# The bilinear MLP's last product summed over four chunks in PSUM, with two small edits of the planner's input

## The chip, the cores and the metric

One NeuronCore of a Trainium2 chip runs the kernel. The metric is the device time of one execution in microseconds, the median of several runs. Five engines work side by side, each through its own list of instructions in order: PE (matrix products), ACT and DVE and POOL (elementwise work), and SP, which here only issues DMAs.

## The reference

Inputs are q, k and v of 4 batches x 8 heads x 576 positions x 64, and phi of 4 x 8 x 576 x 32. The rest are weights. The output has 2304 tokens x 512.

```python
# attention over 32 memory slots
a = softmax of phi over the 576 positions
k_m = einsum('bhsm,bhsd->bhmd', a, k);  v_m = einsum('bhsm,bhsd->bhmd', a, v)
x = softmax(q @ k_m.T / 8) @ v_m               # heads side by side: 2304 x 512
# leaky MLP, 512 -> 2048 -> 512
h = x @ moe_w_in;  y = maximum(0.01 * h, h) @ moe_w_out
# bilinear MLP, 512 -> 1536 -> 512
out = ((y @ moe2_w_a) * (y @ moe2_w_b)) @ moe2_w_out
```

## The kernel before

All large products are fp32 by three passes: each operand is split into a high part (a cast to fp32r) and a low part (what the cast left), and PE multiplies high by high, low by high and high by low, summing in PSUM. So each weight has to be loaded, cleaned up and split before PE can use it, and each intermediate as well.

**A planner writes the order.** Every step is given to `Program.op` with its engines and estimated cost, the tiles that it reads and writes, how early it may be placed (`ahead`), how many places of its room it must leave free (`keep`), and a `slack` that moves its due time. `Program.order` then lists all of them for all engines, a step at a time, and assigns places: "slot" is a common room of SBUF tiles, which raw weights, products, accumulators and stored parts all share; "y" is a room of two PSUM banks. A tile gets its place when the one before it is done with. `SLACK` holds the slacks by kind.

**Stage 1** (to about 393 us) makes the attention and the leaky MLP. At its start SP issues the loads raw_win (first weights), phi, four kv (keys and values of the first batch, 512 of the positions for each half of the heads), kvr (the remaining 64 positions), q, and raw_wout. PE makes `km` from kv and from kvr (line 586), turns the result (`kvt`, 603), makes scores `sc` (674), and then `vw`, `h` (806) and `y` (836).

**Stage 2**, the bilinear MLP, goes through the tokens in two sweeps (s = 0 and 1), in each over 12 chunks c of 128 hidden columns. Tokens that don't fill the halves ("left") are done in the first sweep. For each chunk: raw_wa and raw_wb are loaded (`weight`, line 475), ACT splits off parts (481, 484), DVE cleans and joins them (488, 492, 496, 499), ACT casts the high half of the weight wo (404), DVE or POOL takes off the low half (1004); `w_sums` (987) makes wo number 2 and 3 as sums of them. Chunks 0 to 3 are prepared in stage 1 (`PRE`). All prepared weights are stored to device memory (k_wo, k_wout, and k_wf) and loaded again in the second sweep (1029). With them PE makes the two products for the halves as seven smaller ones (`ab_unit`, tiles abx, aby, abz, line 1049) and for the left tokens as `a` and `b` (`left_unit`, 1100). Their elementwise product is split into p (or pl for the left tokens).

`o_unit` is the last product, p times wout (the tile raw_wout, prepared the same way). One unit takes one quarter of the output columns (e) and one of three token groups (l: 0 and 1 the halves, 2 the left ones), and sums two chunks in one PSUM tile: 6 matmuls (line 1132). The first unit of a group of tokens and columns is copied into an accumulator in SBUF (oacc, oaccl), the others are added there by DVE (1145). After every odd chunk 12 such units go into a queue, from which 6 are placed in each chunk. In the second sweep, chunks below 8 use another form, `o_part` (PE tile os, 1248), which takes sums of wout (w2s, from stored parts wf) and whose first results are copied into osum.

Of the kernel before, what the change touches and what calls it, by code (L numbers as in the profile page):

```python
# [19 lines left out]
P = 128  # L20
# [32 lines left out]
SLACK = {'win0': 5.37, 'wout0': 8.13, 'win': 4.9, 'wout': 4.64, 'wa': 23.6, 'wb': -0.15, 'wout2': 16.8, ('sc', 0, 0): 6.2, ('sc', 0, 1): 3.3, ('sc', 1, 0): 8.05, ('sc', 1, 1): 6.75, ('sc', 2, 0): 11.99, ('sc', 2, 1): 9.96, ('vw', 0, 0): 19.04, ('vw', 0, 1): 7.99, ('vw', 0, 2): 9.35, ('vw', 1, 0): -0.31, ('vw', 1, 1): 19.18, ('vw', 1, 2): 8.18}  # L53
# [279 lines left out]
def tile_mem_attention__leaky_mlp__bilinear_mlp(  # L333
# [128 lines left out]
    def weight(kind, c, k, after=()):  # L462
# [62 lines left out]
        op(two(512), 0, lo, r=[a, ("hi", key)], w=[key], tiles=[cv, key], ahead=any_time, slack=SLACK[kind + "0" if first else kind])  # L525


    def kv_part(b, g):
# [4 lines left out]
        if b == 0:  # L533
            tile_of(phi, "slot", [1, S])
            op("DMA", c_dma(P * S * 4), lambda T: nc.sync.dma_start(T[phi], phiT[b, :, g:g + 1, :]), w=[("e", b, g)], tiles=[phi])
        elif g == 0:
            tile_of(phi, "big", [2, S])
            op("DMA", c_dma(P * S * 8), lambda T: nc.sync.dma_start(T[phi], phiT[b]), w=[("e", b, 0), ("e", b, 1)], tiles=[phi], keep=6)
# [7 lines left out]
        for i, k in enumerate(kvt):  # L546
            tile_of(k, "slot", [2, 512])
            op("DMA", c_dma(P * 4096), lambda T, i=i, k=k: nc.sync.dma_start(T[k], kv[b, g, :, 2 * i:2 * i + 2, :]), w=[k], tiles=[k], keep=6)
        if g == 0:
            tile_of(rest, "slot", [2, 512], parts=64)  # L550
            op("DMA", c_dma(64 * 4096), lambda T: nc.sync.dma_start(T[rest], kv_rest[b]), w=[rest], tiles=[rest], keep=6)
# [96 lines left out]
    def q_load(b, g):  # L648
        if b > 0:
            q = ("q", b, g)  # L650
            tile_of(q, "big", [2, S])
            op("DMA", c_dma(P * S * 8), lambda T: nc.sync.dma_start(T[q], qT[b, g]), w=[q], tiles=[q], keep=6)
            return
        for x in range(2):
            q, cols = ("q", b, g, x), slice(x * NB, (x + 1) * NB)
            tile_of(q, "slot", [2, NB])
            op("DMA", c_dma(P * S * 4), lambda T, q=q, cols=cols: nc.sync.dma_start(T[q], qT[b, g, :, :, cols]), w=[q], tiles=[q])
# [456 lines left out]
    def o_unit(s, c, l, e, pos):  # L1114


        size = NB2 if l < 2 else B * LEFT
        o = ("o", s, c, l, e)
        ps_ = [(("p", s, x, l), 0) if l < 2 else (("pl", c // 2), x % 2) for x in (c, c + 1)]
        ws = [("wout2", x, s) for x in (c, c + 1)]  # L1120
# [8 lines left out]
        def prod(T):  # L1129
            for x, ((g, at), w) in enumerate(zip(ps_, ws)):  # L1130
                for k, (u, v) in enumerate(PASSES):
                    nc.tensor.matmul(  # L1132
                        T[o], T[w][:, u, es], T[g][:, at, v, :], start=(x == 0 and k == 0), stop=(x == 1 and k == 2)
                    )

        op(
            "PE", 6 * c_pass(size), prod,
# [10 lines left out]
        if c == NC2 - 2:  # L1148
# [84 lines left out]
    def o_part(q, x, nth, pos):  # L1233
# [151 lines left out]
```

## Time and profile before

| | us |
|---|---|
| median of the runs shown | 806.5 |
| lowest and highest of 3 | 805.35, 806.81 |
| the profiled execution, its own time | 809.07 |
| span of that profile | 807.3 |
| PE busy | 784.9 |
| DVE busy | 667.7 |
| ACT busy | 375.8 |
| POOL busy | 215.2 |

The mean granted clock of PE in the profile is 0.987 of full speed. Busy times are sums over the span; where PE is full in a stretch, the other engines' idle time there costs nothing. A row of a timeline gives start, length, engine, line, and in brackets how long the engine was idle before and what ended that.

### The profile page before, as it was taken

Reading aid. Unit: us, or ns where it says so; the run is one execution under the profiler, and the core shown is the slowest. Engines: PE = TensorE matmul, PEld = TensorE weight load, DVE = VectorE, ACT = ScalarE, POOL = GpSimd, SP = SyncE. Lnnn points to the kernel's source line nnn. Section 1 sums busy time; section 2 is a strip of 40 time slices with the busy share of each in tenths; the row PEclk is TensorE's granted clock in tenths of the full one; section 3 lists DMA queues with packets and bytes.
Section 4 is the critical chain, followed back from the end, with each engine's and each line's share of the span. In section 5 each row is a group of like instructions: output and inputs, shape, how many; then the busy total and the mean of one; then the engine's idle time right before and its main releaser. Section 6 shows DMA issues by size and latency. Waiting matters only on the chain.

```text
span 807.3 us, 13391 instructions
## 1 busy us (share of the span) xinstructions
PE 784.9 (97%) x4898; PEld 700.0 (87%) x4898; DVE 667.7 (83%) x1273; ACT 375.8 (47%) x817; POOL 215.2 (27%) x328
## 2 busy tenths in 40 slices
PE   5889999999999999999999999999999989999998
PEld 4578889999999999999988888888888878878886
DVE  6898899889887988888768899889885676888975
ACT  5657776777565665654326534344321143222110
POOL 3462247215011411431100113056330000244300
PEclk9789999999999999999999999999999999999999
DMA  9885302064227133136887555646578778957302
GB/s 325 323 281 181 132 1 74 6 235 125 76 76 267 59 132 118 42 125 233 279 311 276 209 199 192 208 158 202 216 264 304 276 267 274 296 173 283 130 1 104
DMA packets 55218, 150.02 MB, mean 186 GB/s; under 512 B 6897, under 2 KB 20209, under 8 KB 55153
## 3 DMA queue, kind: packets, MB, share of 16 engines
q1 hardware_dynamic: 55152, 149.18, 53.4%
q8 instruction: 38, 0.62, 0.3%
q14 instruction: 28, 0.22, 0.1%
HBM read 103.55 MB, written 45.61 MB: 185 GB/s over the span
## 4 chain that ended last, share of the span: by engine, by line
PE 93%; DMA 3%; DVE 2%; issue 1%; ACT 0%; SPq 0%; DVEq 0%; ACTq 0%
PE y L836 26%; PE o L1132 13%; PE h L806 12%; PE aby L1049 12%; PE abz L1049 8%; PE abx L1049 8%; PE os L1248 4%; PE vw L757 2%; PE b L1100 2%; PE a L1100 2%; PE sc L674 1%; DMA kvr<-in_kv_rest_dram 1%; DMA k_wout<-wout 1%; PE km L586 1%; DMA raw_win<-in_w_in_dram 1%
## 5 line engine op out<-in xcount | busy, mean ns | idle before, releaser
L836 PE MATMUL y<-g,wout 128*128 128x288 f32 x1536 | 221.0, 297 | 0.0
L836 PEld LDWEIGHTS y<-g,wout 128*128 128x128 f32 x1536 | 210.8, 190 | 3.7 <-issue 1.7
L1049 PE MATMUL aby<-yb_T,wo 128*128 128x512 f32 x432 | 110.2, 390 | 0.5 <-DVE t L1057 0.5
L1049 PEld LDWEIGHTS aby<-yb_T,wo 128*128 128x128 f32 x432 | 80.1, 188 | 16.8 <-DVE t L1057 0.9
L1132 PE MATMUL o<-p,wout 128*128 128x512 f32 x384 | 94.0, 390 | 0.0
L783 ACT ACTIVATE g<-h 128x288 fp32r<-128x288 f32 x128 | 52.8, 413 | 70.1 <-PE h L806 64.4
L1132 PEld LDWEIGHTS o<-p,wout 128*128 128x128 f32 x384 | 71.9, 188 | 15.4 <-DVE osum L1145 0.3
L806 PE MATMUL h<-ahi,vwh 128*128 128x288 f32 x256 | 76.8, 300 | 1.2 <-ACT ahi L404 1.2
L1057 DVE TENSOR_TENSOR t<-aby,t 128x512 f32<-128x512 f32 x72 | 49.5, 688 | 34.2 <-PE aby L1049 32.4
L806 PE MATMUL h<-alo,vwh 128*128 128x288 f32 x256 | 76.1, 297 | 0.8 <-POOL alo L387 0.8
L806 PE MATMUL h<-ahi,vwl 128*128 128x288 f32 x256 | 75.9, 296 | 0.0
L1049 PE MATMUL abx<-yb_B,wo 128*128 128x512 f32 x288 | 73.4, 390 | 0.0
L1049 PEld LDWEIGHTS abx<-yb_B,wo 128*128 128x128 f32 x288 | 53.4, 188 | 10.6
L848 DVE TENSOR_TENSOR acc<-y,acc 128x288 f32<-128x288 f32 x96 | 43.2, 454 | 19.6 <-PE y L836 18.7
L822 DVE TENSOR_TENSOR g<-t,g 128x288 fp32r<-128x288 f32 x102 | 49.0, 484 | 4.5 <-ACT t L783 4.4
L783 ACT ACTIVATE t<-h 128x288 f32<-128x288 f32 x128 | 52.4, 409 | 0.1
L806 PEld LDWEIGHTS h<-ahi,vwh 128*128 128x128 f32 x256 | 48.4, 189 | 4.2 <-issue 2.6
L806 PEld LDWEIGHTS h<-alo,vwh 128*128 128x128 f32 x256 | 48.6, 190 | 1.3 <-POOL alo L387 1.2
L806 PEld LDWEIGHTS h<-ahi,vwl 128*128 128x128 f32 x256 | 48.5, 189 | 0.0
L387 POOL TENSOR_TENSOR g<-t,g 128x288 fp32r<-128x288 f32 x26 | 26.4, 1017 | 76.0 <-ACT t L783 58.6
L772 DVE TENSOR_TENSOR vwl<-vw,vwh 64x512 fp32r<-64x512 f32 (+1 forms) x64 | 39.8, 622 | 7.4 <-ACT vwh L404 5.9
L404 ACT CAST vwh<-vw 64x512 fp32r<-64x512 f32 (+2 forms) x62 | 31.6, 509 | 23.7 <-PE vw L757 13.8
(328 smaller groups left out, 1472.6 us busy)
## 6 DMA issues: line engine op xcount, KB each, us to landing
k_wo<-wo SPq DMA_DIRECT2D x32, 512.0 KB, 2.9
wo<-k_wo SPq DMA_DIRECT2D x32, 512.0 KB, 4.9
raw_wout<-in_w_out_dram SPq DMA_DIRECT2D x24, 512.0 KB, 4.5
raw_win<-in_w_in_dram SPq DMA_DIRECT2D x16, 512.0 KB, 5.7
kv<-in_kv_dram SPq DMA_DIRECT2D x16, 512.0 KB, 8.5
k_yb_T<-yb_T SPq DMA_DIRECT2D x8, 512.0 KB, 7.9
raw_wa<-in_w_a_dram SPq DMA_DIRECT2D x8, 512.0 KB, 4.3
raw_wb<-in_w_b_dram SPq DMA_DIRECT2D x8, 512.0 KB, 5.9
```

The lines of the kernel that those rows point to most:

```text
L404: nc.scalar.copy(dst, src)
L772: nc.vector.tensor_tensor(T[lk][to, j // 2, cols], T[o][i * 64:(i + 1) * 64, :], T[hk][to, j // 2, cols].bitcast(F32), op=ALU.subtract)
L783: nc.scalar.activation(dst, src, AF.Prelu, alpha=0.01)
L806: nc.tensor.matmul(T[o], T[w[u]][:, k, fs], T[a[v]][:, k, cols], start=(k == 0 and i == 0), stop=(k == 1 and i == 2))
L822: lambda T, e: engines[e].tensor_tensor(T[g][:, i, 1, :], T[t], T[g][:, i, 0, :].bitcast(F32), op=ALU.subtract),
L836: nc.tensor.matmul(T[o], w[:, u, es], g[:, v, :], start=(f == 0 and i == 0), stop=(f == 3 and i == 2))
L848: "DVE", c_dve(NB), lambda T: nc.vector.tensor_tensor(T[acc][:, e, :], T[o], T[acc][:, e, :], op=ALU.add),
L1049: nc.tensor.matmul(T[o], T[w][:, which, u, k * P:(k + 1) * P], T[ys[v]][:, k, :], start=first and k == 0 and x == 0, stop=k == 1 and x == ...
L1057: op("DVE", 0.69, lambda T: nc.vector.tensor_tensor(T[to], T[o], T[x], op=ALU.add), r=[o, x], w=[to], tiles=[o, x, to])
L1100: nc.tensor.matmul(T[o], T[w][:, k // 2, u, k % 2 * P:(k % 2 + 1) * P], T[ys[v]][:, k, :], start=(k == 0 and x == 0), stop=(k == 3 and x = ...
L1132: nc.tensor.matmul(T[o], T[w][:, u, es], T[g][:, at, v, :], start=(x == 0 and k == 0), stop=(x == 1 and k == 2))
L1248: nc.tensor.matmul(T[o], lhs(T, u), T[g][:, v, :], start=k == 0, stop=k == 2)
```

## The change

Three edits. First, in the first sweep `o_unit` sums four chunks in place of two: a unit has 12 matmuls, there are 36 units rather than 72, they enter the queue after chunks 3, 7 and 11, and 3 are placed in each chunk. The second sweep's units stay as they were. Second, the first batch's loads get slacks of their own and kv and kvr no longer have to leave 6 places free. (The slacks of win and wout are split in two, with equal values.) Third, the first copy of `o_part` may go to DVE or ACT at plain cost, without the bias that `copy_by` gives.

```diff
@@ -50,7 +50,7 @@
...
-SLACK = {'win0': 5.37, 'wout0': 8.13, 'win': 4.9, 'wout': 4.64, ...
+SLACK = {'phi0': 0.0, ('kv0', 0): 1.0, ('kv0', 1): 0.0, 'kvr0': 3.0, ('q0', 0): 0.0, ('q0', 1): 0.0, ('win0', 0): 5.37, ('win0', 1): 5.37, ('wout0', 0): 8.13, ('wout0', 1): 8.13, 'win': 4.9, 'wout': 4.64, ...
...
@@ kv_part @@
-            op("DMA", c_dma(P * 4096), lambda T, i=i, k=k: nc.sync.dma_start(T[k], kv[b, g, :, 2 * i:2 * i + 2, :]), w=[k], tiles=[k], keep=6)
+            op("DMA", c_dma(P * 4096), lambda T, i=i, k=k: nc.sync.dma_start(T[k], kv[b, g, :, 2 * i:2 * i + 2, :]), w=[k], tiles=[k], keep=6 if b else 0, slack=0 if b else SLACK["kv0", g])
...
-            op("DMA", c_dma(64 * 4096), lambda T: nc.sync.dma_start(T[rest], kv_rest[b]), w=[rest], tiles=[rest], keep=6)
+            op("DMA", c_dma(64 * 4096), lambda T: nc.sync.dma_start(T[rest], kv_rest[b]), w=[rest], tiles=[rest], keep=6 if b else 0, slack=0 if b else SLACK["kvr0"])
...
@@ o_unit @@
+        xs = range(c, c + (2 if s else 4))
...
-        ps_ = [(("p", s, x, l), 0) if l < 2 else (("pl", c // 2), x % 2) for x in (c, c + 1)]
-        ws = [("wout2", x, s) for x in (c, c + 1)]
+        ps_ = [(("p", s, x, l), 0) if l < 2 else (("pl", x // 2), x % 2) for x in xs]
+        ws = [("wout2", x, s) for x in xs]
...
-                        T[o], T[w][:, u, es], T[g][:, at, v, :], start=(x == 0 and k == 0), stop=(x == 1 and k == 2)
+                        T[o], T[w][:, u, es], T[g][:, at, v, :], start=(x == 0 and k == 0), stop=(x == len(xs) - 1 and k == 2)
...
-            "PE", 6 * c_pass(size), prod,
+            "PE", 3 * len(xs) * c_pass(size), prod,
...
-        if c == NC2 - 2:
+        if c == NC2 - len(xs):
...
@@ o_part @@
-            op(copy_by(NB2, True), 0, lambda T, e: copy(e, part(T, i), T[o]), r=[o], w=[tok(i)], tiles=[o, acc(i)])
+            op({"ACT": c_act(NB2), "DVE": c_dve(NB2)}, 0, lambda T, e: copy(e, part(T, i), T[o]), r=[o], w=[tok(i)], tiles=[o, acc(i)])
...
@@ the loop over chunks @@
-            for i in range({NC2 - 2: 4, NC2 - 1: 1}.get(c, 7) if s else 6):
+            for i in range({NC2 - 2: 4, NC2 - 1: 1}.get(c, 7) if s else 3):
...
-            elif c % 2:
+            elif c % 2 and (s or c % 4 == 3):
...
-                        queue.append(lambda pos, s=s, c=c, l=l, e=e: o_unit(s, c - 1, l, e, pos))
+                        queue.append(lambda pos, s=s, c=c, l=l, e=e: o_unit(s, c - 1 if s else c - 3, l, e, pos))
```

In the rows of the orders below, a tile's name is followed by a number of its own; the number of a chunk is not always part of it. A row's brackets name the engines and DMA queues for which it waits.

**The start, SP.** Before:

```order
L535 DMA phi_0_142<-in_phiT_dram 128x576
L535 DMA phi_1_147<-in_phiT_dram 128x576
L548 DMA kv_0_0_153<-in_kv_dram 128x1024
L548 DMA kv_0_1_159<-in_kv_dram 128x1024
L548 DMA kv_1_0_178<-in_kv_dram 128x1024
L548 DMA kv_1_1_195<-in_kv_dram 128x1024
L551 DMA kvr_206<-in_kv_rest_dram 64x1024
L657 DMA q_0_0_209<-in_qT_dram 128x2x288
```

After:

```order
L535 DMA phi_0_142<-in_phiT_dram 128x576
L535 DMA phi_1_147<-in_phiT_dram 128x576
L551 DMA kvr_153<-in_kv_rest_dram 64x1024
L548 DMA kv_0_0_156<-in_kv_dram 128x1024
L548 DMA kv_0_1_168<-in_kv_dram 128x1024
L548 DMA kv_1_0_189<-in_kv_dram 128x1024
L548 DMA kv_1_1_222<-in_kv_dram 128x1024
L657 DMA q_0_0_230<-in_qT_dram 128x2x288
```

The small load kvr stands ahead of the four kv, where it stood behind them.

**Chunk 8 of the first sweep, SP.** Before, raw_wa_0_6293 and raw_wb_0_6320 are the raw weights of chunk 8; k_wo_6 and k_wo_7 are stores of the prepared weights of chunks 6 and 7:

```order
L475 DMA raw_wout_6_0_6185<-in_w_out_dram 128x512 [waits DVE_49,PE_49,Activation_49]
L475 DMA raw_wout_7_0_6197<-in_w_out_dram 128x512 [waits DMAHW3_49,PE_49]
L1014 DMA k_wo_6_3_6217<-wo_6_3_6138 128x1024 [waits DMAHW4_49]
L1014 DMA k_wo_7_0_6281<-wo_7_0_6220 128x1024 [waits DMAHW5_49,DVE_49]
L475 DMA raw_wa_0_6293<-in_w_a_dram 128x4x128 [waits DMAHW6_49,PE_49]
L475 DMA raw_wb_0_6320<-in_w_b_dram 128x4x128 [waits DMAHW7_49]
L1014 DMA k_wo_7_2_6358<-wo_7_2_6323 128x1024 [waits DMAHW0_49,DVE_49]
L1014 DMA k_wo_7_1_6378<-wo_7_1_6259 128x1024 [waits DMAHW1_49,Pool_49]
L521 DMA k_wf_6409<-cv_wout_6_0_6208 128x512 [waits DMAHW2_49,DVE_49]
L521 DMA k_wf_6409<-cv_wout_7_0_6240 128x512 [waits DMAHW3_49,DVE_49]
```

After, raw_wa_0_6444 and raw_wb_0_6468 are those of chunk 8, the next pair those of chunk 9, and the last row is chunk 10's raw_wa:

```order
L1014 DMA k_wout_5_0_6335<-wout_5_0_6301 128x1024 [waits DMAHW0_49,DVE_49]
L475 DMA raw_wout_7_0_6355<-in_w_out_dram 128x512 [waits DMAHW1_49,DMAHW7_49,DVE_49,PE_49]
L1014 DMA k_wout_6_0_6377<-wout_6_0_6325 128x1024 [waits DMAHW2_49]
L521 DMA k_wf_6323<-cv_wout_7_0_6390 128x512 [waits DMAHW3_49,DVE_49]
L475 DMA raw_wa_0_6444<-in_w_a_dram 128x4x128 [waits DMAHW4_49,PE_49]
L475 DMA raw_wb_0_6468<-in_w_b_dram 128x4x128 [waits DMAHW5_49]
L475 DMA raw_wa_0_6489<-in_w_a_dram 128x4x128 [waits DMAHW6_49,PE_49]
L475 DMA raw_wb_0_6503<-in_w_b_dram 128x4x128
L475 DMA raw_wa_0_6519<-in_w_a_dram 128x4x128 [waits DMAHW0_49]
```

Chunk 8's pair stood among the stores of chunks 6 and 7 and ahead of all stores of their wout (k_wf, k_wout); it now stands behind the loads of wout 4 to 7 and nearly all of these stores, directly ahead of chunk 9's pair. What raw_wa waits for on PE is the unit o_0_2_3 of the left tokens, the last of the first group of four chunks. That unit and what PE has next, in the order after, the first row of each product:

```order
L1133 MATMUL o_0_2_3_6427<-pl_5653,wout_3_0_5538 128x256 x3
L1049 MATMUL aby_7_6380<-yb_T_0_0_4972,wo_7_3_6110 128x512 [waits DVE_49]
...
L1100 MATMUL a_6453<-yl_4644,wo_7_0_6054 128x256
...
L1100 MATMUL b_6473<-yl_4644,wo_7_1_6093 128x256
...
L1049 MATMUL aby_7_6380<-yb_T_0_0_4976,wo_7_1_6093 128x512 [waits DVE_49]
...
L1049 MATMUL abz_7_6410<-yb_B_0_0_4769,wo_7_3_6110 128x512 [waits DVE_49]
...
L1049 MATMUL abx_8_6545<-yb_B_0_0_4416,wo_8_0_6530 128x512 [waits Activation_49]
```

Of the products before abx_8, the first to use chunk 8's weight wo_8_0, each has 6 matmuls, and a and b have 12. On ACT, in the order after, the same place is:

```order
L404 COPY oaccl<-o_0_2_3_6427 128x256 [waits PE_49]
L481 ACTIVATE cv_wa_0_6471<-raw_wa_0_6444 128x512 [waits DMAHW4_49]
L484 ACTIVATE cv_wa_0_6471<-raw_wa_0_6444 128x512
L481 ACTIVATE cv_wb_0_6498<-raw_wb_0_6468 128x512 [waits DMAHW5_49]
L484 ACTIVATE cv_wb_0_6498<-raw_wb_0_6468 128x512
L404 CAST pl_6345<-pt_6486 128x256 [waits DVE_49]
L481 ACTIVATE cv_wa_0_6514<-raw_wa_0_6489 128x512 [waits DMAHW6_49,PE_49]
L484 ACTIVATE cv_wa_0_6514<-raw_wa_0_6489 128x512
L481 ACTIVATE cv_wb_0_6523<-raw_wb_0_6503 128x512 [waits DMAHW7_49]
L404 CAST wo_8_0_6530<-cv_wa_0_6471 128x2x256 [waits DVE_49,Activation_49]
```

Raw weights of chunk 9 (raw_wa_0_6489, raw_wb_0_6503) are taken up ahead of the cast of wo_8_0.

**The early second sweep.** ACT before, around the copies of osum (os_0_5 is the PE tile that is copied):

```order
L404 COPY osum_7869<-os_0_7_7855 128x512 [waits PE_49]
L404 CAST w_1_0_7888<-w2s_7871 128x2x256 [waits DMAHW4_49,DVE_49,Activation_49]
L404 COPY osum_7869<-os_1_7_7877 128x512 [waits PE_49]
L404 CAST w_1_1_7901<-w2s_7871 128x2x256 [waits DMAHW0_49,Pool_49]
L404 CAST pb_B_7908<-pf_7891 128x512 [waits DVE_49]
L404 COPY osum_7920<-os_0_5_7897 128x512 [waits DMAHW1_49,PE_49]
L404 COPY osum_7920<-os_1_5_7904 128x512 [waits PE_49]
```

DVE after, around the one copy that is there now:

```order
L1178 TENSOR_TENSOR w2s_7736<-wf_7715 128x256 [waits DMAHW7_49,DVE_49]
L1178 TENSOR_TENSOR w2s_7736<-wf_7715 128x256
L1057 TENSOR_TENSOR t_1_2_7745<-aby_2_7671,t_1_2_7669 128x512 [waits PE_49]
L1178 TENSOR_TENSOR w2s_7736<-w2s_7736,wf_7715 128x256 [waits DVE_49]
L1057 TENSOR_TENSOR t_1_2_7745<-abz_2_7695,t_1_2_7745 128x512 [waits DVE_49]
L1188 TENSOR_TENSOR w_1_0_7766<-w2s_7736,w_1_0_7766 128x2x256 [waits Activation_49]
L1057 TENSOR_TENSOR t_1_2_7669<-aby_2_7671,t_1_2_7669 128x512 [waits PE_49]
L1188 TENSOR_TENSOR w_1_1_7777<-w2s_7736,w_1_1_7777 128x2x256 [waits DMAHW1_49,Activation_49]
L1073 TENSOR_TENSOR pf_7795<-abx_2_7652,t_1_2_7669 128x512 [waits DVE_49]
L1057 TENSOR_TENSOR t_1_2_7702<-abz_2_7695,t_1_2_7702 128x512 [waits PE_49]
L406 COPY osum_7810<-os_0_5_7797 128x512 [waits PE_49]
```

The copy of os_0_5 stood on ACT behind the cast w_1_1, and stands on DVE now. The sums w2s of wf stand ahead of the add t_1_2 <- aby_2.

## Rows read from the trace of the kernel before

**Rows 1.** Busy us by stretch: PE, PEld, DVE, ACT, POOL, granted clock, DMA share, GB/s.

```profile
440.00:480.00 40.00, 40.00 (x212) 34.51 (x211) 35.52 (x64) 21.38 (x42) 6.45 (x9) 1.00 0.55 201
640.00:680.00 40.00, 37.83 (x171) 30.79 (x170) 24.80 (x41) 16.03 (x28) 0.74 (x1) 1.00 0.80 267
```

**Rows 2.** What PE waited for, whole run: total us, times, longest.

```profile
PE km L586 <- DMA kvr<-in_kv_rest_dram: 2.5, 1, 2.5
PE kvt L603 <- DVE kvn L595: 2.4, 1, 2.4
PE os L1248 <- ACT osum L404: 2.2, 2, 1.5
PE aby L1049 <- DVE t L1057: 0.5, 1, 0.5
```

**Rows 3.** DVE by line, 393 to 640 us: count, busy us, mean ns.

```profile
L1145 DVE TENSOR_TENSOR oacc<-o,oacc 128x512 f32<-128x512 f32 x40 | 27.5, 688 | 9.6 <-PE o L1132 8.9
L1145 DVE TENSOR_TENSOR oaccl<-o,oaccl 128x256 f32<-128x256 f32 x18 | 7.5, 419 | 4.7 <-PE o L1132 4.6
```

**Rows 4.** Chain of waits in the first sweep: start, us, what, matmuls.

```profile
...
450.60 1.44 PE a L1100 x12
...
455.53 1.43 PE b L1100 x12
...
495.62 1.39 PE abx L1049 x6
```

**Rows 5.** Timeline of SP, ACT and DVE: loads of chunks 4 and 8.

```profile
414.49 0.38 SPq L475 DMA_DIRECT2D raw_wa<-in_w_a_dram  x1
...
416.08 0.43 SPq L475 DMA_DIRECT2D raw_wb<-in_w_b_dram  x1
...
454.17 0.38 SPq L475 DMA_DIRECT2D raw_wa<-in_w_a_dram  x1
...
423.09 0.66 ACT L484 ACTIVATE cv_wb<-raw_wb 128x512 int32<-128x512 uint32 x1 [2.20 <-DMA raw_wb<-in_w_b_dram]
...
427.18 0.63 ACT L404 CAST wo<-cv_wa 128x512 fp32r<-128x512 f32 x1 [1.35 <-issue]
...
428.34 0.68 DVE L1004 TENSOR_TENSOR wo<-cv_wa,wo 128x512 fp32r<-128x512 f32 x1
```

**Rows 6.** Time to landing, loads raw_wa and then raw_wb.

```profile
DMA to landing us min/median/max: 3.6/4.3/6.4
...
DMA to landing us min/median/max: 4.6/5.9/7.2
```

**Rows 7.** Timeline of PE and chain of waits at the start.

```profile
17.67 0.45 PE L586 MATMUL km<-kvr,en 64*32 64x128 f32 x8 [2.50 <-DMA kvr<-in_kv_rest_dram]
18.05 1.93 PE L586 MATMUL km<-kv,en 128*32 128x128 f32 x32
...
48.47 5.06 PE L836 MATMUL y<-g,wout 128*128 128x288 f32 x24
...
7.31 10.32 DMA kvr<-in_kv_rest_dram
```

**Rows 8.** Stretches of 2 us at the start, columns as in rows 1.

```profile
16.00:18.00 2.00, 0.33 (x8) 0.15 (x8) 1.40 (x4) 0.00 (x0) 0.00 (x0) 0.98 1.08 309
18.00:20.00 2.00, 2.00 (x40) 1.46 (x40) 0.48 (x1) 0.00 (x0) 0.00 (x0) 0.50 1.03 413
...
26.00:28.00 2.00, 2.00 (x11) 2.00 (x11) 1.43 (x5) 0.44 (x2) 2.00 (x4) 0.50 1.04 416
...
36.00:38.00 2.00, 2.00 (x10) 1.48 (x11) 2.00 (x3) 1.27 (x4) 1.08 (x1) 0.50 0.67 270
```

**Rows 9.** Timeline of PE and chain of waits, early second sweep.

```profile
664.70 0.98 PE L1248 MATMUL os<-pb_B,wout 128*128 128x512 f32 x3 [1.50 <-ACT osum L404]
...
654.96 9.02 DMA k_wout<-wout
```

**Rows 10.** Time to landing, loads wf.

```profile
DMA to landing us min/median/max: 4.6/5.5/6.2
```

More of the change, by code (lines that the diff above doesn't have):

```diff
@@ L52 @@
 LEAD = 12
-SLACK = {'win0': 5.37, 'wout0': 8.13, 'win': 4.9, 'wout': 4.64, 'wa': 23.6, 'wb': -0.15, 'wout2': 16.8, ('sc', 0, 0): 6.2, ('sc', 0, 1): 3.3, ('sc', 1, 0): 8.05, ('sc', 1, 1): 6.75, ('sc', 2, 0): 11.99, ('sc', 2, 1): 9.96, ('vw', 0, 0): 19.04, ('vw', 0, 1): 7.99, ('vw', 0, 2): 9.35, ('vw', 1, 0): -0.31, ('vw', 1, 1): 19.18, ('vw', 1, 2): 8.18}
+SLACK = {'phi0': 0.0, ('kv0', 0): 1.0, ('kv0', 1): 0.0, 'kvr0': 3.0, ('q0', 0): 0.0, ('q0', 1): 0.0, ('win0', 0): 5.37, ('win0', 1): 5.37, ('wout0', 0): 8.13, ('wout0', 1): 8.13, 'win': 4.9, 'wout': 4.64, 'wa': 23.6, 'wb': -0.15, 'wout2': 16.8, ('sc', 0, 0): 6.2, ('sc', 0, 1): 3.3, ('sc', 1, 0): 8.05, ('sc', 1, 1): 6.75, ('sc', 2, 0): 11.99, ('sc', 2, 1): 9.96, ('vw', 0, 0): 19.04, ('vw', 0, 1): 7.99, ('vw', 0, 2): 9.35, ('vw', 1, 0): -0.31, ('vw', 1, 1): 19.18, ('vw', 1, 2): 8.18}
 START = 17.4
@@ L524, in weight @@
         op(copy_by(512), 0, hi, r=[a], w=[("hi", key)], tiles=[cv, key], ahead=any_time)
-        op(two(512), 0, lo, r=[a, ("hi", key)], w=[key], tiles=[cv, key], ahead=any_time, slack=SLACK[kind + "0" if first else kind])
+        op(two(512), 0, lo, r=[a, ("hi", key)], w=[key], tiles=[cv, key], ahead=any_time, slack=SLACK[(kind + "0", k // 2) if first else kind])
     def kv_part(b, g):
@@ L534, in kv_part @@
             tile_of(phi, "slot", [1, S])
-            op("DMA", c_dma(P * S * 4), lambda T: nc.sync.dma_start(T[phi], phiT[b, :, g:g + 1, :]), w=[("e", b, g)], tiles=[phi])
+            op("DMA", c_dma(P * S * 4), lambda T: nc.sync.dma_start(T[phi], phiT[b, :, g:g + 1, :]), w=[("e", b, g)], tiles=[phi], slack=SLACK["phi0"])
         elif g == 0:
@@ L656, in q_load @@
             tile_of(q, "slot", [2, NB])
-            op("DMA", c_dma(P * S * 4), lambda T, q=q, cols=cols: nc.sync.dma_start(T[q], qT[b, g, :, :, cols]), w=[q], tiles=[q])
+            op("DMA", c_dma(P * S * 4), lambda T, q=q, cols=cols: nc.sync.dma_start(T[q], qT[b, g, :, :, cols]), w=[q], tiles=[q], slack=SLACK["q0", x])
     NM = NB // 32
```

## The prediction

> **What bounds the kernel now.** I read the busy times by stretch first, then what TensorE waited for, then the transfers and the chain of waits.
>
> The busy times say where a saving can count. In 440 to 480 us, in the middle of the first sweep, PE is busy for 40.00 of 40 us at clock 1.00, while DVE is busy for 35.52 [rows 1]. PE is the bound there, and DVE has some 11% of air. In 640 to 680, where the second sweep begins, PE has 37.83 of 40 us. The list of waits names all that PE lost to others in the whole run, in order of size: 2.5 us for the transfer kvr at the start, 2.4 for kvn, 2.2 for the copies osum on ACT, 0.5 for an add of DVE [rows 2]. Small as they are, only these can be won back, and a new PE wait costs its full length wherever PE is full. So the question for each edit is not how much work it saves but whether it shortens or makes a wait of PE.
>
> **Part 1: four chunks in one PSUM sum.** The matmuls stay the same, since three passes over each chunk are needed whether two or four are summed. The 72 units become 36; 8 and 4 of them start an accumulator by a copy, as before, so of 40 adds of 128x512 and 20 of 128x256 there stay 16 and 8. At 688 and 419 ns [rows 3] this is 24 x 0.688 + 12 x 0.419 = 21.5 us of DVE. What it brings: nothing. These adds run beside a PE that is full in these stretches [rows 1], and in the first sweep the list has no row in which PE waits for an oacc add [rows 2]. It would pay only if DVE were late for PE, and the one DVE wait of this kind is 0.5 us in the second sweep. I take 0, with 0.5 as the most.
>
> The price is in the buffers. The products p and pl and the weights wout of four chunks now stay in their slots until the last unit of the group, and the slots are one common room: the raw weights of a later chunk come into the places that these leave. In the new order on SP, the load of chunk 8's raw_wa stands behind all of the loads and stores of the second weights (wout) of chunks 4 to 7 and waits for PE's last unit of the first group, o of the left tokens. From the end of that unit to the first matmul that uses chunk 8's weights, PE has only this to do: three products of six matmuls, one a and one b. That is 3 x 1.39 + 1.44 + 1.43 = 7.04 us [rows 4], and this is the time in which the load has to be issued, land, and be split.
>
> How long does that take? Chunk 4 of the old kernel shows it in full: raw_wa issued at 414.49, raw_wb at 416.08; ACT starts on raw_wb at 423.09 as it lands; the high half of wo is cast at 427.18 and the low half is taken off at 428.34 for 0.68, so at 429.02 it is done [rows 5]. From the issue of raw_wa that is 14.5 us, and from the landing of raw_wb 5.9. Chunk 8 in the old kernel was issued at 454.17 [rows 5] and first used at 495.62 [rows 4], 41 us later, so none of this was seen. Now for the bounds. The shortest: raw_wa lands after its least time, 3.6 [rows 6], raw_wb has no part in it, and 5.9 follows: 9.5, so PE waits 9.5 - 7.0 = 2.5. The longest is the 14.5 of chunk 4: 7.5 (some of its time was ACT busy with other things). Between them: in the new order ACT also has to take up raw_wa and raw_wb of chunk 9 before it casts chunk 8's first wo, and these are issued about 3 us later, since they wait for product a of chunk 7. Then raw_wb of chunk 9 is issued at about 3.5, lands 5.9 later (its median [rows 6]) at 9.4, ACT splits off a first part (0.66 [rows 5]) to 10.1, and the cast takes 0.63 to 10.7, with the low half 0.68 behind, 11.4. I take this, 11.5 - 7.0 = **4.5 us** of wait at the first product of chunk 8. What is behind it (b of chunk 8, then chunk 9) has a further 4 us of PE work in front and I count nothing for it.
>
> Then the clock. At the start of the old kernel PE idled 2.50 us for kvr, and the granted clock, still 0.98 in 16 to 18 us, is 0.50 in the five stretches of 2 us from 18 to 28 [rows 7, 8]: the lower of its two levels, 1.2 GHz in place of 2.4. In the second sweep a wait of 1.50 us [rows 9] left it at 1.00 [rows 1]. A wait of 4.5 lies beyond the one that lowered it. Of the three times at half clock that the start shows, the one from 18 to 28 is the longest, with a PE that went on pausing; the shortest has one whole stretch, 36 to 38 [rows 8]. A full PE loses half of such a time, so 1 to 5 us. PE is full here, so I go by the shorter, with its edges some 4 us, and take **2.0**; without a drop it is 0.
> The Trainium skill (TensorE: Matmul & The Clock Gate, "Why this matters for your kernels") warns of this: a gap between bursts of matmuls sends the array back to its low clock. By that rule the 2.0 is due; the row of 2.50 us agrees with it.
>
> **Part 2: kvr ahead of kv.** kvr is issued at 7.31, behind four loads kv, and lands 10.32 us later [rows 7]; PE waits for it until 17.67, and then still has 0.45 of km's kvr part and 1.93 and more of the next km [rows 7]. In the new order kvr comes first and the last of the kv loads is last. All bytes still land at about 17.6, since the queue is the same length, but of km only the part of the last load is left then, so km ends 1.3 to 2.0 us earlier. Against this, DVE has about 0.4 us more to do before the first y (the low part of one more wout comes to it from POOL). y starts at 48.47 [rows 7]; the clock's half stretches lie in other places. I take **-2.0**, from 0 (kvn, on DVE, is late anyway [rows 2]) to -3.5 (if one half-clock stretch gets shorter).
>
> **Part 3: the first osum copy by DVE or ACT alike.** One copy goes from ACT to DVE, and in the new order none of them stands behind the ACT cast that waited for a slot: in the old kernel the slot's store, k_wout, was issued at 654.96 and took 9.02, and PE got its 1.50 us wait of it [rows 9], with 0.68 before it: 2.2 [rows 2]. I count these as gone. In their place DVE now has sums of stored weights (w2s) ahead of an add that PE waits for, and these wait for the load wf, which is released about 6.1 us of PE work ahead; it lands after 4.6 to 6.2 [rows 10], and 0.8 of sums and 0.7 of add follow, so PE waits 0 to 1.6 there; I take 0.8. Together **-1.4**, from -2.2 to +0.3. The loads at the start of the second sweep come closer too: the first wo is issued some 6 us before its use, by order; a landing of the size of wf's [rows 10] makes that 0 to 3 us, I take **+0.4**.
>
> **Rivals.**
> (a) The wait at chunk 8 without a drop of the clock: everything as above less 2.0. For it: waits of up to 1.50 left the clock alone, and this PE was full before. Sum +1.5: 808.0.
> (b) The wait is at its lower bound or hidden, because ACT doesn't need chunk 9's loads to land late (a 3.6 us landing), and the start pays: 0 to 2.5 - 2.0 - 1.4 + 0.4 = -3.0 to -0.5; taken at -2.5: 804.0. For it: PE had no wait for raw_wa anywhere in the old kernel [rows 2]. It is the case of a faster kernel, and it decides at a wait below some 1.4 us.
> (c) The shortage of slots repeats. The second group's end falls at the change of sweeps, and if the loads of the second sweep wait as chunk 8's do, another 4.5 comes in place of the 0.4: +7.6, 814.1. It speaks against it that the second sweep loads finished weights, with nothing to convert.
> The Trainium skill (Perfetto Trace Analysis, "Optimization Strategy") says that a gap which repeats on the engine that should be full can mean too little SBUF for the next tile; by it this is the case to fear. No run here shows it yet.
> (d) The edit doesn't do what it says to the time: PE full, adds hidden, waits swapped for one another. 806.5 within 0.2%.
>
> **How the numbers follow.** The profiled execution took 809.07, its span 807.3; the three timed runs have a median of 806.5. The changes are sums of microseconds of PE, so I add them to the median. Forecast: -2.0 + 4.5 + 2.0 - 1.4 + 0.4 = +3.5, **810.0 us**. Chances: forecast 0.38, (a) 0.20, (b) 0.24, (c) 0.10, (d) 0.08. A measurement of this kernel can tell some 0.2% from no change, 1.6 us: below 804.9 is faster, above 808.1 slower. Case (b) is faster in 0.22 of its 0.24, (a) lies on the border, half in same and half in slower, (d) is same, the forecast and (c) are slower. So faster 0.22; same 0.10 + 0.08 + 0.02 = 0.20; slower 0.38 + 0.10 + 0.10 = 0.58. The range: 803.5, into (b), to 815.0, which holds (c) and the forecast with a wait at its longest (7.5 in place of 4.5, and 4 in place of 2 for the clock).
>
> **What would show it.** PE's list of waits should lose kvr, or most of it, and the osum row, and have a new one at line 1049, first product of chunk 8 at about 490 us, for ACT's wo, of 2.5 to 7.5 us; behind it the clock should read 0.50 for 2 or more 2-us stretches. The start of y should be near 46.5. DVE's busy time should be some 20 us lower with no gain from it. The forecast is wrong if raw_wa of chunk 8 is issued 12 us or more before its first matmul, or if that matmul has no wait; and if the time falls below 805 by the start alone.

## The result: slower by half a per cent, and where

| | median, us | lowest to highest | runs |
|---|---|---|---|
| before | 807.23 | 805.35 to 810.35 | 9 |
| changed | 811.91 | 809.25 to 816.09 | 9 |

The ratio of changed to before is 1.0052, with a 95% interval of 1.0035 to 1.0070: slower, by about 4 us. The profiled execution of the changed kernel took 809.25 with a span of 807.5 and is the fastest of its nine; the one of before took 809.07 with a span of 807.3, which is above its median. So the two traces alone show almost no difference, while the medians differ by 4.7 us (4.2 by the ratio). Both have to be explained.

What PE waited for in the changed kernel, whole run (total us, times, longest), to be read beside [rows 2]:

```profile
PE abx L1049 <- ACT wo L404: 3.0, 1, 3.0
...
PE vw L736 <- DVE vwl L745: 1.4, 1, 1.4
PE kvt L603 <- DVE kvn L595: 1.4, 2, 1.2
...
PE abx L1049 <- DVE wo L1004: 0.4, 1, 0.4
PE os L1249 <- ACT osum L404: 0.3, 1, 0.3
```

The wait for kvr is gone from the list and the one for osum is down from 2.2 to 0.3; a new one of 3.0 + 0.4 stands at abx. Another new one, 1.4 for DVE's vwl, stands at 60 us, behind the first loads, and takes back part of what kvr gave. The timeline of PE shows the wait at abx, at the first product of chunk 8 (start, us, engine, line, tiles, matmuls, idle before):

```profile
512.06 1.60 PE L1100 MATMUL a<-yl,wo 128*128 128x256 f32 x12
...
516.32 1.52 PE L1049 MATMUL abz<-yb_B,wo 128*128 128x512 f32 x6
520.87 0.73 PE L1049 MATMUL abx<-yb_B,wo 128*128 128x512 f32 x2 [3.02 <-ACT wo L404]
521.99 1.47 PE L1049 MATMUL abx<-yb_B,wo 128*128 128x512 f32 x4 [0.39 <-DVE wo L1004]
523.25 2.77 PE L1100 MATMUL a<-yl,wo 128*128 128x256 f32 x12
525.81 1.71 PE L1049 MATMUL abx<-yb_B,wo 128*128 128x512 f32 x6
```

A second cost is in the row at 523.25: the twelve matmuls of this a take 2.77 us, where those of the a at 512.06 took 1.60. The stretches of 2 us show why (columns as in rows 1):

```profile
520.00:522.00 2.00, 0.74 (x3) 0.31 (x3) 2.00 (x5) 1.81 (x4) 1.57 (x3) 1.00 0.88 344
522.00:524.00 2.00, 2.00 (x8) 1.74 (x9) 2.00 (x4) 1.27 (x3) 0.70 (x2) 0.69 0.64 260
524.00:526.00 2.00, 2.00 (x11) 2.00 (x11) 1.90 (x4) 0.70 (x2) 2.00 (x3) 0.50 0.07 27
526.00:528.00 2.00, 2.00 (x13) 1.72 (x12) 1.62 (x3) 0.81 (x2) 2.00 (x3) 0.96 1.01 408
```

The granted clock goes to 0.50 behind the wait and comes back at about 526.

**A way to compare runs.** Three instants on PE have the same amount of matmul work before and behind them in all these kernels (2900 or 2901, then 1321 or 1322, then 625 or 626 matmuls in every profile, and 12 more in the one with the filled wait): the last y unit (end of the first MLP), the first os unit (in the second sweep), and the final run of o units. Their starts split a run into the start, the first sweep and what follows. In the changed kernel:

```profile
390.50 1.75 PE L836 MATMUL y<-g,wout 128*128 128x288 f32 x12
...
648.57 0.84 PE L1249 MATMUL os<-pb_B,wout 128*128 128x512 f32 x3
...
791.12 12.69 PE L1133 MATMUL o<-p,wout 128*128 128x512 f32 x54
```

and before:

```profile
393.10 1.75 PE L836 MATMUL y<-g,wout 128*128 128x288 f32 x12
...
645.67 0.84 PE L1248 MATMUL os<-pb_B,wout 128*128 128x512 f32 x3
...
790.93 12.70 PE L1132 MATMUL o<-p,wout 128*128 128x512 f32 x54
```

The differences of these starts, for one profile of each kernel that ran, with the ratio of the timed runs:

| kernel | start | first sweep | second sweep | ratio to before (95%) |
|---|---|---|---|---|
| before | 393.10 | 252.57 | 145.26 | 1 |
| changed | 390.50 | 258.07 | 142.55 | 1.0052 (1.0035 to 1.0070) |
| changed, again | 392.83 | 260.20 | 142.63 | 1.0057 (1.0039 to 1.0074) |
| four-chunk sum alone | 393.19 | 259.19 | 144.60 | 1.0066 (1.0046 to 1.0087) |
| first loads alone | 391.46 | 252.68 | 143.57 | 0.9983 (0.9964 to 1.0001) |
| osum copy alone | 391.84 | 252.57 | 143.70 | 0.9992 (0.9975 to 1.0010) |
| both small edits, no sum | 389.76 | 252.56 | 144.12 | 0.9965 (0.9949 to 0.9982) |
| four units a chunk | 390.26 | 258.90 | 144.46 | 1.0048 (1.0030 to 1.0066) |
| wait filled with matmuls | 389.88 | 259.26 | 142.36 | 1.0023 (1.0010 to 1.0037) |
| sum of three chunks | 391.16 | 252.53 | 143.05 | 0.9976 (0.9961 to 0.9990) |
| all, wout's slack 0 | 390.45 | 253.25 | 141.44 | 0.9939 (0.9920 to 0.9958) |
| the same, again | 389.89 | 252.66 | 141.44 | 0.9937 (0.9918 to 0.9956) |
| small edits, wout's slack 0, no sum | 390.62 | 252.59 | 145.02 | 0.9980 (0.9966 to 0.9994) |
| sum and wout's slack 0 only | 393.78 | 252.50 | 141.44 | 0.9972 (0.9957 to 0.9988) |

In the first sweep 252.5 is a floor, at which PE is busy all the time, and before already has it: nothing could be won there. The change loses 5.5 there, and wins 2.6 at the start and 2.7 in the second sweep: +0.2, as the two spans say. The table also shows what one profile can't: the start of a kernel varies by 2 us and more from run to run (390.50 and 392.83 for the very same kernel). Over all of them, the four kernels with the old first loads have 391.84 to 393.78, 393.0 in the mean, and the ten profiles with the new ones 389.76 to 392.83, 390.7 in the mean.

### The profile page after: what moved, and what is told of

It is laid out like the page before. It is cut to its first block, busy times and chain, and to the rows that moved or that the text cites. A ratio compares the mean times of both kernels' runs of the same rounds, so it can differ in the third digit from the quotient of the medians.

```text
span 807.5 us, 13290 instructions
## 1 busy us (share of the span) xinstructions
PE 784.1 (97%) x4898; PEld 700.3 (87%) x4898; DVE 659.3 (82%) x1258; ACT 375.9 (47%) x811; POOL 173.4 (21%) x277
## 4 chain that ended last, share of the span: by engine, by line
PE 90%; DMA 6%; DVE 2%; SPq 1%; issue 1%; ACT 0%; DVEq 0%; ACTq 0%
PE y L836 26%; PE o L1133 13%; PE h L806 12%; PE aby L1049 11%; PE abx L1049 8%; PE abz L1049 7%; PE os L1249 4%; PE vw L757 2%; PE a L1100 2%; PE b L1100 2%; DMA raw_wout<-in_w_out_dram 1%; DMA kv<-in_kv_dram 1%; DMA k_wout<-wout 1%; DMA kvr<-in_kv_rest_dram 1%; PE sc L674 1%; DMA out_dram<-oacc 1%
## 5 line engine op out<-in xcount | busy, mean ns | idle before, releaser
L1133 PE MATMUL o<-p,wout 128*128 128x512 f32 x384 | 91.4, 390 | 0.0
L404 ACT CAST p<-t 128x512 fp32r<-128x512 f32 x30 | 18.6, 621 | 58.9 <-DVE t L1078 26.5
```

What stands on the lines that cost most here:

```text
L404: nc.scalar.copy(dst, src)
L1133: nc.tensor.matmul(T[o], T[w][:, u, es], T[g][:, at, v, :], start=(x == 0 and k == 0), stop=(x == len(xs) - 1 and k == 2))
```

## The experiments

### Each part alone

The theory: the four-chunk sum makes chunk 8's weights late, which costs the wait and the clock, and the small edits each give their own bit. The rivals: the start's gain is an accident of one profile; DVE's saved adds pay after all; the lateness costs more in other runs.

The first loads alone (the new slacks and `keep`, sums of two):

```diff
...
-... w=[rest], tiles=[rest], keep=6)
+... w=[rest], tiles=[rest], keep=6 if b else 0, slack=0 if b else SLACK["kvr0"])
...
```

> Only the slacks and free places of the first batch's loads are changed; sums stay at two chunks. Theory (each edit has its own effect, and the start gains what the changed kernel's profile shows, y at 44.8 in place of 48.5 us): 3.6 us faster than before, at least 1.5, with the kvr row gone from PE's list of waits. Rival (the start's gain is an accident of where the clock's low stretches fall in one profile, and typical runs do not have it): within 1.5 us of before.

Measured: 806.81 against 808.50, ratio 0.9983, its interval reaching 1.0001. In its profile the wait for kvr is gone, another of 0.6 us for kv is there, and those for kvn add up to 2.9 in place of 2.4. By the ratio it is 1.4 us, at the edge of what can be told from no change and just under the 1.5 that the theory gave as its least: by this run it is the rival that stands, and the 3.6 of the one profile was in part an accident.

The four-chunk sum alone:

```diff
...
-        ws = [("wout2", x, s) for x in (c, c + 1)]
+        ws = [("wout2", x, s) for x in xs]
...
```

> Only the four-chunk sum of the first sweep; start and osum copies as before. Theory: raw_wa of chunk 8 is issued only some 7 us of PE work ahead of its first use, PE waits 3 to 4 us there and then runs at half clock for some 3.5 us (1.7 lost), and the start and the copies keep their old waits: 5 us slower than before, ratio 1.006. Rival 1 (the changed kernel's profile was a lucky run and the wait is longer in others): 7 to 10 us slower. Rival 2 (fewer adds on DVE pay somewhere): under 3 us slower.

Measured: 813.29 against 808.50, ratio 1.0066, 5.3 us. The theory said 5. The first sweep takes 259.19, 6.6 over the floor, with the wait of 3.36 for ACT's wo at chunk 8 and half clock behind it, and a wait of 2.24 for osum in the second sweep.

The osum copy alone:

```diff
-            op(copy_by(NB2, True), 0, lambda T, e: copy(e, part(T, i), T[o]), ...
+            op({"ACT": c_act(NB2), "DVE": c_dve(NB2)}, 0, lambda T, e: copy(e, part(T, i), T[o]), ...
```

> Only the first copy of the second sweep's parts may go to DVE or ACT at plain cost. Theory: it takes away PE's two waits for ACT's osum copies, 2.2 us in the profile of before, and adds at most 0.5 elsewhere: 1.5 us faster, ratio 0.998. Rival: the waits move (the slot that the store of wout held up is late for another step as well) and it is within 0.7 us of before.

Measured: 807.21 against 808.50, ratio 0.9992, not to be told from none. Its profile has 0.6 us of the osum wait left of 2.2, and the second sweep is 1.6 shorter, so the mechanism is there in the trace at the size expected; the timed runs don't resolve it.

The product of the three ratios is 1.0041, the whole change 1.0052 and 1.0057: within the intervals, the effects add.

### Is the wait at chunk 8 the whole price?

First, the group of four done sooner, by placing four units a chunk:

```diff
-            for i in range({NC2 - 2: 4, NC2 - 1: 1}.get(c, 7) if s else 3):
+            for i in range({NC2 - 2: 4, NC2 - 1: 1}.get(c, 7) if s else 4):
```

> The whole change, but four units of the queue a chunk in place of three in the first sweep, so that a group of four chunks is done after three and chunk 8's raw weights are issued some 17 us of PE work ahead of their first use in place of 7. Theory (the wait at chunk 8 and the clock drop behind it are the whole price of the four-chunk sum): no PE wait at chunk 8, no low clock there, 5 us faster than the changed kernel and 4 to 5 faster than before. Rival (the sum costs elsewhere too, by the slots that it holds): still at before's time or above, with new waits of PE.

Measured: 812.00 against 808.50, ratio 1.0048. The wait at chunk 8 is gone, as its order of loads should give, and the kernel is as slow as with it. The theory's number fell and its rival's stands. Its first sweep takes 258.90, with two waits for ACT's copy t: 1.14 at 408.28 and 2.27 at 436.13, with half clock behind the second; in the second sweep it has one of 2.3 for osum. PE's timeline and ACT's, at 432 to 436:

```profile
432.34 1.52 PE L1049 MATMUL abz<-yb_T,wo 128*128 128x512 f32 x6
436.13 2.03 PE L1049 MATMUL abx<-yb_B,wo 128*128 128x512 f32 x6 [2.27 <-ACT t L1060]
...
433.66 0.66 ACT L484 ACTIVATE cv_wb<-raw_wb 128x512 int32<-128x512 uint32 x1 [3.95 <-DMA raw_wb<-in_w_b_dram]
434.97 0.62 ACT L404 CAST p<-t 128x512 fp32r<-128x512 f32 x1 [0.66 <-DMA k_yb_T<-yb_T]
435.50 0.58 ACT L1060 COPY t<-abx 128x512 f32<-128x512 f32 x1
```

ACT stands still for 3.95 us until a raw weight has landed, then again until a store has left its slot, and the copy t, which frees the PSUM bank that PE wants, is behind both. From 385 to 440 us SP's loads of line 475 wait for 12.0 us in all until stores k_yb_T have left their slots. The weight here is chunk 5's, and PE is only at chunk 3 and waits for its copy. So the price isn't tied to chunk 8: it is a load that comes late because the slots are taken, in front of an engine that works in order, and an edit that helps one chunk can hand it to another.

Second, the same room, but another order: the slack of the second weights, which made their loads for chunks 4 to 7 go ahead of chunk 8's first weights, set to 0:

```diff
-... 'wa': 23.6, 'wb': -0.15, 'wout2': 16.8, ...
+... 'wa': 23.6, 'wb': -0.15, 'wout2': 0, ...
```

> The whole change, with one number more: the slack of the second weights (wout2) is 0 in place of 16.8, so that their loads for chunks 4 to 7 no longer go ahead of chunk 8's raw_wa and raw_wb, which are issued some 40 us of PE work ahead of their use. Theory (who gets the scarce slots decides; the load's lateness is the price): no PE wait at chunk 8 and no low clock there, 5 us faster than the changed kernel, some 1 to 2 faster than before (ratio 0.998). Rival (with four chunks held, the slots are too few whatever the order, as in the run with four units a chunk, where the wait moved to chunks 5 and 6): a new wait of 2 us or more in the first sweep, and no faster than before.

Measured: 802.99 against 807.71, ratio 0.9939: 4.7 us faster than before, more than the theory said, and 9 faster than the changed kernel. Once more:

> The whole change with the slack 0 of the second weights, once more. If what the first run of it showed holds (the wait at chunk 8 is gone and the second sweep has no wait for osum): ratio 0.994, below 0.9965, and in the profile no wait of PE over 0.6 us behind 60 us. If the first was a lucky set of six runs: 0.9965 to 0.998, as the small edits alone and as the slack without the sum.

802.43 against 807.13, ratio 0.9937. Chunk 8's raw_wa is now issued 39.8 us ahead of the first product of that chunk, which has no wait. Behind 60 us PE has none left at all. The last wait, the load and the product are

```profile
59.80 0.51 PE L736 MATMUL vw<-win,vp_hi 128*128 128x256 f32 x2 [1.40 <-DVE vwl L745]
...
477.27 0.39 SPq L475 DMA_DIRECT2D raw_wa<-in_w_a_dram  x1
...
517.08 1.52 PE L1049 MATMUL abx<-yb_B,wo 128*128 128x512 f32 x6
```

and the first sweep takes 252.66, the floor. (In the profile of this kernel's first run the first sweep has one wait, 0.5 for an add of DVE, and takes 253.25.) So the four-chunk sum doesn't need more room than there is. It needs the room in another order.

Third, a smaller group:

```diff
-        xs = range(c, c + (2 if s else 4))
+        xs = range(c, c + (2 if s else 3))
...
-            elif c % 2 and (s or c % 4 == 3):
+            elif c % 2 if s else c % 3 == 2:
...
```

(with four units a chunk.)

> The whole change, but sums of three chunks in place of four, four units a chunk. Chunk 8's raw weights are issued some 41 us ahead again; the shortest lead is that of chunk 9, 21 us. Theory: no wait for raw weights, so as fast as the two small edits without the sum, 0.9975; the 16 us of DVE adds saved bring nothing. Rival (fewer adds pay once the wait is gone): 2 us or more faster than the two small edits alone.

Measured: 805.93 against 807.71, ratio 0.9976; the first sweep is at 252.53. It is as the theory said.

### The clock, apart from the wait

To part the clock from the wait, the wait was filled: twelve matmuls on data that are there, into a PSUM tile that nothing reads.

```diff
...
+        def prod(T):
+            for n in range(12):
+                nc.tensor.matmul(
+                    T[o], T[w][:, which, 0, 0:P], T[ys[0]][:, 0, :], start=n == 0, stop=n == 11, ...
...
+        op("PE", 12 * c_pass(NB2), prod, ..., tiles=[o, w, *ys], pos=(step, -1))
```

> The whole change, with 12 matmuls of 512 columns more on PE ahead of chunk 8's first product, into a PSUM tile that nothing reads (2.7 us of work put into the 3.4 us wait). Theory (the wait sends the clock down and that costs 1.7 us beside the wait itself): PE waits under 1 us there, the clock stays at 1.00, and the kernel is 1.5 us faster than the changed one although it does more. Rival (the clock drop costs nothing, since DVE or ACT set the pace behind the wait): as fast as the changed kernel, or 1 to 3 us slower if the added work delays anything.

Measured: 809.86 against 807.71, ratio 1.0023, beside 1.0052 and 1.0057 without the filling: the kernel that does 2.7 us more on its bound engine is about 2.5 us faster. PE's timeline and one stretch of its clock there:

```profile
518.66 2.88 PE L1095 MATMUL idle<-yb_B,wo 128*128 128x512 f32 x12
521.74 0.73 PE L1049 MATMUL abx<-yb_B,wo 128*128 128x512 f32 x2 [0.20 <-ACT wo L404]
522.99 1.20 PE L1049 MATMUL abx<-yb_B,wo 128*128 128x512 f32 x4 [0.52 <-DVE wo L1004]
524.03 1.58 PE L1114 MATMUL a<-yl,wo 128*128 128x256 f32 x12
525.45 1.55 PE L1049 MATMUL abx<-yb_B,wo 128*128 128x512 f32 x6
...
522.00:524.00 2.00, 1.48 (x6) 0.89 (x6) 2.00 (x4) 1.43 (x3) 1.10 (x2) 1.00 0.39 155
```

The clock stays at 1.00, and from the start of a to the next product it is 1.42 us, where the changed kernel took 2.56 (523.25 to 525.81). In the changed kernel's timeline, the starts from 521.99 to 527.36 lie 0.35 + 1.13 + 0.19 = 1.67 us further apart than at 0.227 us a matmul of 512 columns and 0.119 of 256; here they don't. That is the clock's part, 1.7 of the 5.5. From the end of abz by its pace (516.32 + 1.36, and 518.66 here) to the second abx it is 8.13 us in the changed kernel and 6.79 with the filling: 1.3 us less in this place, close to the theory's 1.5, while the timed runs say 2.3 to 2.7. In the first sweep of this one profile, 259.26, the gain is covered by two other waits, 1.26 for the copy t at 408.02 and 0.91 for a load of stored weights wo at 598.28.

### Does the sum itself bring anything?

Three kernels part the sum from the slack: both small edits without the sum, the same with the slack, and the sum with the slack but without the small edits. The first has no slack edit; the others have

```diff
+... 'wout2': 0, ...        (both small edits; sums of two chunks)
```

> The two small edits (first loads, osum copy) without the four-chunk sum. Theory: effects add up, -1.4 and -0.7 us as measured apart, so 2 us faster than before, ratio 0.9975, with no wait in the first sweep. Rival (they get in each other's way): no faster than before.

> The two small edits and the slack 0 of the second weights, with sums of two chunks. Theory (four chunks in PSUM bring nothing themselves; the gain of the run with the slack 0 over the small edits alone comes from the slack): 0.994, as fast as the same with the four-chunk sum. Rival (with its wait gone, the four-chunk sum pays, by fewer adds or by an order in which the second sweep has no wait): 0.9965, as fast as the small edits alone, 2 us slower than with the sum.

```diff
+... 'wout2': 0, ...        (sums of four chunks; first loads and osum copy as before)
```

> The four-chunk sum and the slack 0 of the second weights, without the two small edits. Theory (the price of the sum is the lateness of chunk 8's load alone): no wait at chunk 8, 0.998 to 1.000, 6 us faster than the sum alone. Rival (the small edits are needed for it): a new wait, over 1.002.

The two small edits without the sum: 805.61 against 807.71, 0.9965. With the slack besides: 805.08 against 807.11, 0.9980, so the slack isn't what wins. With the sum and the slack, 0.9939 and 0.9937, outside both their intervals (though the interval of 0.9939, to 0.9958, reaches into that of 0.9965). The sum and the slack without the small edits: 804.82 against 807.11, 0.9972. So the theory that four chunks in PSUM bring nothing fell: with its lateness cured the sum is worth 0.3 to 0.4%, 2 to 3.5 us. The table says where: not in the first sweep, where all are at 252.5, but in the second, 141.44 in all three kernels with sum and slack, against 143.6 to 145.3 without the sum. Those without it have PE waits for osum there. In the run with both small edits and the slack but no sum, the chain of waits has

```profile
639.66 9.24 DMA k_wo<-wo
...
649.27 5.04 DMA k_wo<-wo
...
654.40 0.59 ACT osum L404
...
655.03 1.66 PE os L1248 x6
```

a store that holds a slot, as [rows 9] show for before. With the sum and the slack the stores of the first sweep's end are placed otherwise and nothing waits for one; with the sum alone there is still the wait of 2.24. That the wait is for a slot and not for an add speaks for the order as the cause. Whether the adds that DVE no longer has play a part, no run here parts.

### The changed kernel once more

> The changed kernel as it is, once more, so that it stands beside the other runs of this call and leaves a second profile. Theory (the wait at chunk 8 and its clock are 5 us in every run; the profile seen so far was the fastest of nine runs, and others have one more wait, of ACT for a load or a store at 400 to 440 us as in the run with filled wait): ratio 1.005, again a wait of 3 to 4 us at chunk 8, and perhaps a wait of abx for ACT's copy t before 440 us. Rival (the first profile shows all there is): no other new wait of PE over 0.5 us in the first sweep.

811.62 against 807.11, ratio 1.0057. This profile is of the slowest of the six runs (813.81, span 812.0), as the first one was of the fastest of its nine, so the two lie on either side of the medians of 811.6 and 811.9. It has the wait at chunk 8 (3.68) and 1.65 us of clock behind it, and one that the first profile didn't have. The chain of waits:

```profile
400.86 7.81 DMA raw_wa<-in_w_a_dram
408.76 0.66 ACT cv_wa L481
409.42 0.56 ACT cv_wa L484
409.99 0.51 ACT p L404
410.49 0.49 ACT t L1060
411.02 1.66 PE abx L1049 x6
```

Chunk 4's raw_wa, too, stands on ACT ahead of the copy t that PE needs, and is not there yet. In the first profile it was issued 6.34 us after the start of the last y unit and ACT had it 6.73 later, at 403.57, and there was no wait; here it was issued 8.03 after that start and ACT had it 7.90 later, and PE waited 1.30. The filled kernel, with the same order of loads, has it as well (1.26). So in this order the time rides on when a load is issued and how fast it lands, and a run can be 1 to 2 us better or worse by it. With that and the start's spread, the two profiles, 4.5 us apart, fit.

## Right and wrong, step by step

**The forecast** was +3.5 us; the ratio says +4.2. Its parts fared like this.

- *Adds hidden, worth 0.* Right for the changed kernel and for the first sweep of all of them: 16 adds of 128x512 are left of 40 and the floor of 252.5 doesn't move. Not right as a rule: with the load in time, the sum gains 2 to 3.5 us in the second sweep, a place where the prediction didn't look for it. The sign that it named, some 20 us less work on DVE, didn't come either. DVE's busy time fell from 667.7 to 659.3, and POOL's from 215.2 to 173.4:

```profile
PE 784.1 (97%) x4898; PEld 700.3 (87%) x4898; DVE 659.3 (82%) x1258; ACT 375.9 (47%) x811; POOL 173.4 (21%) x277
```

  The planner used most of the time that the adds left on DVE for work that POOL had done.
- *The wait at chunk 8, 4.5.* Right in its chain, at another time than the one named. The load at 454.17 and the product at 495.62, taken for chunk 8's [rows 4, 5], are chunk 6's: 252 matmuls of line 1049, those of six chunks, stand before that product. Chunk 8's in before are

```profile
492.83 0.38 SPq L475 DMA_DIRECT2D raw_wa<-in_w_a_dram  x1
...
534.12 1.55 PE L1049 MATMUL abx<-yb_B,wo 128*128 128x512 f32 x6
```

  which are 41 us apart too, so by luck nothing in the sum changes; only the place, 520.87 in the changed kernel, isn't "about 490". In the changed kernel the unit o of the left tokens ends at 510.7; SP and ACT then show

```profile
510.87 0.38 SPq L475 DMA_DIRECT2D raw_wa<-in_w_a_dram  x1
...
513.69 0.37 SPq L475 DMA_DIRECT2D raw_wa<-in_w_a_dram  x1
514.11 0.50 SPq L475 DMA_DIRECT2D raw_wb<-in_w_b_dram  x1
...
514.52 0.68 ACT L481 ACTIVATE cv_wa<-raw_wa 128x512 f32<-128x512 f32 x1 [3.27 <-DMA raw_wa<-in_w_a_dram]
...
519.64 0.68 ACT L481 ACTIVATE cv_wb<-raw_wb 128x512 f32<-128x512 f32 x1 [0.80 <-DMA raw_wb<-in_w_b_dram]
520.21 0.61 ACT L404 CAST wo<-cv_wa 128x512 fp32r<-128x512 f32 x1
```

  The issue comes 0.2 after the unit, chunk 9's pair 3.0 after it, and the cast of wo is done 10.1 after it, where the sum had 10.7. The wait, with what pipelining hides in the rows, is 3.19 + 0.67 = 3.9 us (the starts of the rows against their pace). The term was a little large, because the low half's lateness costs PE only what it hasn't spent on the high one.
- *The clock, 2.0.* Right: 1.7 in both profiles of the changed kernel by the paces, which the filled run bears out, and 2.6 in that of the sum alone. The rule of the Trainium skill (TensorE: Matmul & The Clock Gate, "Why this matters for your kernels") that was weighed there holds for these waits of 3.0 to 3.7; the last section has shorter ones that went either way.
- *The start, -2.0.* The mechanism is right: the last km, the one from kvr, ended at 20.57 in before (first row) and at 18.62 in the changed kernel (second row; 19.27 in its second profile), 1.95 and 1.30 earlier, as the term had it.

```profile
19.92 0.65 PE L586 MATMUL km<-kvr,en 64*32 64x128 f32 x8
...
18.20 0.42 PE L586 MATMUL km<-kvr,en 64*32 64x128 f32 x8
```

  What becomes of it is less even. The wait of 1.4 for vwl at 60 us, which the prediction didn't see, is in all ten profiles with the new first loads and in none of the four with the old; and the half-clock stretches lie elsewhere (18 to 28 in before [rows 8], 32 to 38 in the changed kernel). The size is right for the average (-2.3 in the means of the table, -1.4 by the timed runs of the edit alone) and was luck for any one run: -3.7 at the first y in one profile (44.82 in place of 48.47 [rows 7]), -2.6 at the last y, -0.3 in the second profile.
- *The second sweep, -1.4 and +0.4.* The osum waits went, as forecast, but for 0.3 (0.9 in the second profile). The new wait that was put against them, for w2s behind wf, did not come: DVE began the sums at 657.26, and PE has no wait there. Nor did the one for the second sweep's first wo, except in the filled run (0.9). The stretch won 2.7 in place of 1.0, and this is the term with the largest miss.
- *What was missed.* The wait for chunk 4's load, 1.3 us in two of the four profiles with this order. The prediction looked at raw weights only as something that PE's own products wait for. It didn't ask what stands behind the same load on ACT: a copy that frees a PSUM bank.
- *The sum.* Set against the profile of before, the two profiles of the changed kernel give in the mean -1.4 at the start, +6.6 in the first sweep (5.5 of it at chunk 8 in both, the rest mostly chunk 4's wait in one) and -2.7 in the second: +2.5, where the forecast had -2.0 + 6.5 - 1.0 = +3.5. The profiled execution of before, 809.07, is itself 1.8 above the median of the nine runs, and that brings the +2.5 to the measured +4.2. Why it lies so high no run shows, since there is one profile of before. So the mechanism was right, and that the number came as close as 0.7 is in part luck.
- *A reading that was too wide.* [rows 2] is a part of the list, and its waits aren't all that PE lost. The longest one in before is

```profile
PE ta L569 <- ACT phi L556: 5.1, 1, 5.1
```

  and 5.9 us more in waits of 0.2 to 2.2 are left out, at the start as well. No term of the sum hangs on them.

**The rivals.** (a), the wait without a drop of the clock, is out by the rows. (b), the wait at its bound, is out: 3.0 to 3.7 in all three profiles of this order that weren't filled. (c), a shortage that shows again at the change of sweeps, didn't come there; but its idea was nearer to the truth than its place. The shortage does repeat, at chunk 4's load and, when four units are placed a chunk, at chunk 5's. (The Trainium skill's sentence on repeating gaps, in Perfetto Trace Analysis, "Optimization Strategy", points the right way as far as the gaps go. The cause that it names as possible, too little room, doesn't hold here: with the loads in another order the same 24 slots suffice.) (d), no change, is out by the interval.

## What to carry to other kernels

- An edit that saves work beside a full engine can still decide the time, by how long it holds buffers. Before making a group larger, find which load takes the places that the group frees, and count the bound engine's work between that release and the load's first use; here 7 us against the 10 that a load and its conversion take.
- When such a lead is too short, look at who else gets the room first. A later due time for loads that aren't urgent made the same change 0.6% faster than before in place of 0.5% slower.
- An engine that works in order turns a late load into a late everything: look behind the load on its queue, not only at who uses its data. And split runs at instants of equal work; one profile's total can hide a loss of 5 us behind gains of 5.

## What the hardware showed unexpectedly

Waits of about one length did not do the same to the clock. In the run with four units a chunk, the wait of 2.27 us at 436.13 was followed by half clock (first row below), and the one of 2.34 at 674.43 in the same run was not (second row); before it PE had been busy alike. The waits of 3.02, 3.36 and 3.68 at chunk 8 were followed by half clock each time.

```profile
438.00:440.00 2.00, 2.00 (x6) 1.61 (x5) 1.76 (x4) 0.50 (x1) 0.00 (x0) 0.50 1.02 418
...
676.00:678.00 2.00, 2.00 (x11) 1.65 (x10) 0.00 (x0) 0.61 (x2) 0.00 (x0) 1.00 0.87 354
```

And the same kernel ran 1% apart from one execution to the next (before: 803.99 to 812.34 in 27 runs), of which the profiles show the start and the landings of single loads as parts; what else is in it stays open.
